# Seven weight loads move from SP's DMA queue to GpSimd's, in a kernel whose order is set by a planner

## The chip, the cores and the metric

One core of one Trainium2 chip. The metric is the device time of one execution in microseconds; the kernel before takes 885.57 us (median of three runs, 884.84 to 885.59).

## The reference, cut to what matters

```python
# q, k, v: (8 batches, 8 heads, 576 positions, 64); w_in: (512, 2048); w_out: (2048, 512); all float32
scores = scale * np.matmul(q_c, k_c.transpose(0, 1, 2, 4, 3))      # chunks of 64 positions
scores = scores - np.max(scores, axis=-1, keepdims=True)
attn = np.exp(scores)
attn = attn / (np.sum(attn, axis=-1, keepdims=True) + 1e-09)
x = np.matmul(attn, v_c)                                           # then to (4608 tokens, 512)
h = x @ w_in
g = np.maximum(h, 0.0) + np.log1p(np.exp(-np.abs(h)))              # softplus
return g @ w_out
```

## The kernel before, in words

The 4608 tokens are 36 pairs of chunks (128 tokens each), and four pairs make an m-tile of 512 tokens; there are nine. Each m-tile runs 16 blocks, one for each 128 of the 2048 hidden columns. Block g has a first GEMM G1_g (x times w_in, 12 matmuls, line 527), softplus and a split of the result into a high and a low part (`sp`, `hi`, `lo`: ACT at lines 538 and 542, then DVE or POOL at line 546), and a second GEMM G2_g (12 matmuls, line 560). TensorE (PE) runs them as G1_0, G1_1, G2_0, G1_2, G2_1 and so on. A float32 product is made of three matmuls over high and low parts, so the weights are split too.

A weight unit u is 128 hidden columns of w_in or of w_out: units 0 and 1 are w_in of blocks 0 and 1, and then they alternate (unit 2 is w_out of block 0, unit 3 w_in of block 2, unit 4 w_out of block 1, and so on). Each of the 32 units takes this way: `load` (512 KB by DMA, lines 228 and 233) into one of three `raw` buffers; `w_top` (ACT or POOL, line 239) and `w_low` (ACT, line 248), which read the raw buffer and free it; `w_add` (DVE, line 253); `w_hi` (ACT or POOL, line 274); `w_lo` (DVE or POOL, line 278). A w_in unit has to be ready for G1 of its block, a w_out unit for G2.

Attention is made in two ways. The first four pairs (`q0` to `v3`, line 305, with PE transposes) come ahead of G1_0, which needs `xl3`, the last of them (DVE, line 507). The others come in bursts of PE work between blocks: B3, B8 and B15 in the first m-tile, in two halves each, then two bursts in each m-tile. A burst needs for its two pairs q and k (line 404, eight DMAs of 32 KB each, then DVE transposes `Tq`, `Tk` at line 412), and for the pairs before it `v` (line 314, four DMAs) and `swap` (line 445, eight DMAs from SBUF to SBUF, after softmax).

The order on every engine is fixed when the program is built, and each engine works through its own list and waits at an entry until what this needs is there. The class `Plan` sets the order: it plays the tasks through with a cost for each, and at each moment takes the task with the lowest `urg`. All DMAs before go through SP's queue. They take eight semaphores in turn, so a DMA on SP also waits until the eighth before it has landed; the planner before knows this only as at most five loads under way (`FLYING`).

```python
LOAD_AFTER = "v0"                       # when the first weight load may be ordered
can = [t for t in wait[eng] if ready[t["name"]] <= now + 1e-9 and has_room(t, now)]
t = min(can, key=lambda t: (t["urg"], t["seq"]))
before = dict(zip(seq[1:], seq))        # PE: G1_g follows G2_(g-2), or the burst
```

Of the kernel before, what the change touches and what calls it, by code (L numbers as in the profile page):

```python
# [16 lines left out]
F16 = mybir.dt.float16  # L17
# [16 lines left out]
class Plan:  # L34
# [6 lines left out]
    FLYING = 5  # L41
# [6 lines left out]
    def add(  # L48
        self, name, eng, cost, fn, needs=(), urg=0.0, table=None, take=(), kb=0, slack=0.0, after=(), port=False
    ):  # L50
        self.tasks[name] = dict(
            name=name, eng=eng, cost=cost, fn=fn, needs=list(needs) + list(after), after=set(after), urg=urg, table=table,
            take=take, kb=kb, slack=slack, seq=len(self.tasks), port=port or eng == "POOL",
        )

    def order(self):
# [7 lines left out]
        wait, flying = {}, []  # L64
# [28 lines left out]
        while times:  # L93
# [3 lines left out]
            flying = [e for e in flying if e > now]  # L97
# [45 lines left out]
def chunked_attention_softplus_ffn(  # L143
# [92 lines left out]
    def w_top(u):
        top = tops[u % TOP_BUFS].bitcast(F16).rearrange("p (f t) -> p f t", t=2)[:, :, 1]
# [340 lines left out]
    T0, TG = 18.0, 5.5  # L578
    TK = (0,2)
# [33 lines left out]
    for u, (g, is_in, fc) in enumerate(units):  # L613
# [23 lines left out]
        plan.add(last[0], ph_, 0.65 if ph_ == "POOL" else 0.53, partial(w_hi, u, is_in, fc),  # L637
# [39 lines left out]
    for at, (pv, ps) in bursts.items():  # L677
# [19 lines left out]
        for i in (a, b):  # L697
            for n, src in (("q", q), ("k", k)):
# [6 lines left out]
                plan.add(f"{n}{i}", "SP", 4.2, partial(blk_load, i, n, src), free, urg=d - QK_URG, kb=256,  # L705
# [4 lines left out]
        for n in range(2):  # L710
            i = a + n
            free = [] if ps == F else [nxt[n]]
            plan.add(f"v{i}", "SP", 2.8, partial(blk_v_load, i), free, urg=d - V_URG, kb=256,
# [11 lines left out]
            plan.add(f"swap{i}", "SP", 5.0, partial(blk_swap, i), [f"Te{i}"] + gone, urg=d - SW_URG, kb=256)  # L725
# [68 lines left out]
```

## Time and profile before

| what | value |
|---|---|
| median of three runs | 885.57 us |
| the profiled execution | 883.88 us |
| its span, first to last instruction | 882.0 us |
| PE busy in the span | 861.7 us (98%) |
| ACT, DVE, POOL busy | 316.8, 329.8, 56.1 us |
| mean granted TensorE clock | 0.998 |
| moved by DMA | 63.91 MB, 72 GB/s over the span |

The profiled execution is 1.69 us below the median; 1.9 us of it lie outside the span. Busy shares are means over the whole span: the first 130 us, in which the weights are loaded and split, have other limits than the rest.

### The profile page before, as it was taken

How to read it: one execution, taken by the hardware profiler on the slowest of the kernel's cores; microseconds unless marked ns; L12 is line 12 of the kernel's file. 1: busy time of each engine (PE TensorE's matmuls, PEld its weight loads, DVE VectorE, ACT ScalarE, POOL GpSimd, SP SyncE). 2: the span in 40 equal slices, each digit the busy share in tenths (PEclk: the TensorE clock that was granted, in tenths of full speed). 3: DMA queues.
4: the chain of work that ended last, by engine and by line, in shares of the span. 5: the costliest groups of instructions: out<-in, count | busy, mean ns of one | idle time of the engine just before them, and what ended most of it. 6: DMA issues, size and time to landing. Idle time of an engine off the chain costs nothing.

```text
span 882.0 us, 14812 instructions
## 1 busy us (share of the span) xinstructions
PE 861.7 (98%) x5868; PEld 700.9 (79%) x5868; DVE 329.8 (37%) x550; ACT 316.8 (36%) x494; POOL 56.1 (6%) x58
## 2 busy tenths in 40 slices
PE   8699989999999999999999999999999999999998
PEld 7577878888888888888888888888888888888886
DVE  5667854333415251524233432334153414121111
ACT  4677763232424242324232422333232423232222
POOL 1353630000000000000000000000000000000000
PEclk9999999999999999999999999999999999999999
DMA  9676763313232324132412232232223231000001
GB/s 224 171 200 201 208 149 92 62 39 63 41 86 40 63 41 100 28 64 41 105 30 46 52 62 74 41 66 42 81 39 63 44 94 31 18 18 31 1 1 48
DMA packets 214852, 63.91 MB, mean 72 GB/s; under 512 B 191744, under 2 KB 208128, under 8 KB 214784
## 3 DMA queue, kind: packets, MB, share of 16 engines
q1 hardware_dynamic: 214784, 62.98, 31.7%
q8 instruction: 46, 0.75, 0.4%
q14 instruction: 22, 0.18, 0.1%
HBM read 45.09 MB, written 9.44 MB: 62 GB/s over the span
## 4 chain that ended last, share of the span: by engine, by line
PE 87%; DMA 6%; SPq 2%; ACT 2%; POOL 1%; issue 1%; DVE 1%; DVEq 0%; ACTq 0%; POOLq 0%
PE po L560 43%; PE pa L527 41%; DMA raw<-in_moe_w_out_dram 3%; PE pa L491 2%; DMA raw<-in_moe_w_in_dram 2%; PE pa L424 2%; SPq L305 1%; DMA q<-in_q_dram 1%; ACT top L239 0%; SPq L228 0%; POOL top L239 0%; ACT low L248 0%; ACT u L538 0%; DMA k<-in_v_dram 0%; DVE low L253 0%
## 5 line engine op out<-in xcount | busy, mean ns | idle before, releaser
L538 ACT ACTIVATE u<-pa 128x512 f32<-128x512 f32 x144 | 86.0, 597 | 498.5 <-PE pa L527 498.4
L546 DVE TENSOR_TENSOR g_lo<-u,g_hi 128x512 fp32r<-128x512 f32 x136 | 94.6, 695 | 356.7 <-ACT g_hi L542 356.3
L527 PE MATMUL pa<-x,wib 128*128 128x512 f32 x864 | 208.7, 390 | 1.9 <-DVE wib L278 1.9
L527 PEld LDWEIGHTS pa<-x,wib 128*128 128x128 f32 x864 | 161.6, 188 | 38.1 <-DVE wib L278 2.3
L527 PE MATMUL pa<-x,wi_hi 128*128 128x512 f32 x576 | 178.0, 390 | 1.4 <-DVE x L507 1.4
L560 PE MATMUL po<-late,g_hi 128*128 128x512 f32 x540 | 172.1, 394 | 0.0
L527 PEld LDWEIGHTS pa<-x,wi_hi 128*128 128x128 f32 x576 | 108.1, 188 | 24.1 <-DVE x L507 1.8
L560 PEld LDWEIGHTS po<-late,g_hi 128*128 128x128 f32 x540 | 101.2, 187 | 24.4
L560 PE MATMUL po<-wo_hi,g_lo 128*128 128x512 f32 x288 | 115.6, 401 | 3.1 <-DVE g_lo L546 3.1
L560 PE MATMUL po<-late,g_lo 128*128 128x512 f32 x288 | 114.6, 398 | 0.0
L560 PE MATMUL po<-wo_lo,g_hi 128*128 128x512 f32 x288 | 114.4, 397 | 0.0
L560 PE MATMUL po<-wo_hi,g_hi 128*128 128x512 f32 x288 | 113.8, 395 | 0.0
L527 PE MATMUL pa<-x,wi_lo 128*128 128x512 f32 x288 | 112.8, 392 | 0.0
L542 ACT CAST g_hi<-u 128x512 fp32r<-128x512 f32 x144 | 89.2, 619 | 4.4
L560 PEld LDWEIGHTS po<-wo_hi,g_lo 128*128 128x128 f32 x288 | 54.4, 189 | 16.5 <-DVE g_lo L546 3.3
L527 PEld LDWEIGHTS pa<-x,wi_lo 128*128 128x128 f32 x288 | 54.0, 188 | 14.1 <-PE po L560 2.8
L560 PEld LDWEIGHTS po<-wo_hi,g_hi 128*128 128x128 f32 x288 | 54.4, 189 | 13.4
L560 PEld LDWEIGHTS po<-wo_lo,g_hi 128*128 128x128 f32 x288 | 54.4, 189 | 12.8
L560 PEld LDWEIGHTS po<-late,g_lo 128*128 128x128 f32 x288 | 54.0, 187 | 13.1
L455 DVE TENSOR_REDUCE mx<-pa 128x8 f32<-128x512 f32 x32 | 22.0, 686 | 70.0 <-ACT x L503 68.5
L412 DVE STREAM_TRANSPOSE ka<-k 128x512 f32<-128x512 f32 x30 | 21.3, 710 | 52.8 <-DMA k<-in_k_dram 42.5
L471 DVE TENSOR_REDUCE den<-qe 128x8 f32<-128x512 f32 x32 | 21.1, 660 | 16.6 <-ACT qe L466 16.6
(97 smaller groups left out, 546.0 us busy)
## 6 DMA issues: line engine op xcount, KB each, us to landing
out_dram<-raw SPq DMA_DIRECT2D x36, 256.0 KB, 2.6
raw<-in_moe_w_in_dram SPq DMA_DIRECT2D x16, 512.0 KB, 4.6
raw<-in_moe_w_out_dram SPq DMA_DIRECT2D x16, 512.0 KB, 4.5
eT<-ka SPq DMA_DIRECT2D x256, 32.0 KB, 1.9
q<-in_q_dram SPq DMA_DIRECT2D x240, 32.0 KB, 2.1
k<-in_k_dram SPq DMA_DIRECT2D x240, 32.0 KB, 2.1
q<-in_v_dram SPq DMA_DIRECT2D x60, 64.0 KB, 2.4
k<-in_v_dram SPq DMA_DIRECT2D x60, 64.0 KB, 2.4
```

The lines of the kernel that those rows point to most:

```text
L305: eng.dma_start(dst[p0 : p0 + rows], src[b, :, s0 : s0 + rows, :].rearrange("h s d -> s h d"))
L412: nc.vector.transpose(t, live.pop((n, i)))
L424: nc.tensor.matmul(pa[o, c2, col : col + C], qT[r, a * HP + hl, :], kT[r, a * HP + hl, :], start=True, stop=True,)
L455: nc.vector.tensor_reduce(mx, sc, axis=AX.X, op=ALU.max)
L471: nc.vector.tensor_reduce(den, e, axis=AX.X, op=ALU.add)
L491: nc.tensor.matmul(pa[o, a, col : col + C], vt[r, 4 * j + 2 * h2 + c2, :], eT(r, c2, j, h2), start=True, stop=True,)
L527: nc.tensor.matmul(ph, wt[:, c, fs], x[:, :, c, :], start=(n == 0), stop=(n == 3 * KC - 1))
L538: nc.scalar.activation(w["u"], w["ph"], AF.Softplus)
L542: nc.scalar.copy(w["hi"], w["u"])
L546: (nc.gpsimd if pool else nc.vector).tensor_tensor(w["lo"], w["u"], w["hi"].bitcast(F32), op=ALU.subtract)
L560: nc.tensor.matmul(pos[w["m"]][t], gg[:, ts_], wt, start=(w["first"] and n == 0), stop=(w["last"] and n == 2),)
```

## The change

Units 2, 3, 4, 5, 7, 9 and 11 are loaded by a DMA that POOL (GpSimd) issues, on a queue of its own with semaphores of its own; the other 25 stay on SP. No load is ordered ahead of `v3` now (before: `v0`). The planner models the main queue anew: eight lanes, in which a DMA waits until the eighth before it has landed, each of the several DMAs of a task by itself (`parts`), and a limit on how far issues run ahead of the data (`AHEAD`). Costs and due times of many tasks are set anew, and with them the lists of who does which part of a unit. The two `top` buffers are handed out in the order of use. The second burst of the later m-tiles comes at block 14 (before 13).

```diff
-    FLYING = 5
+    FLYING = 8
+    AHEAD = 3.2
...
-                if free.get(eng, 0.0) > now + 1e-9 or eng == "SP" and len(flying) >= self.FLYING:
+                if free.get(eng, 0.0) > now + 1e-9:
...
+                last = end
+                if t["kb"]:
+                    end, lanes = now, landed.setdefault(eng, [0.0] * self.FLYING)
+                    for _ in range(t["parts"]):
+                        end = max(end, lanes[-self.FLYING] + 0.1, dma_free - self.AHEAD) + cost / t["parts"]
+                        dma_free = max(end + 1.0, dma_free) + t["kb"] * 1024 / self.RATE / t["parts"]
+                        lanes.append(max(dma_free + 0.8, end + 1.6))
+                    last = lanes[-1]
...
-                if t["kb"]:
-                    dma_free = max(now + 1.8, dma_free) + t["kb"] * 1024 / self.RATE
-                    end = max(dma_free + 0.8, end + 2.0)
-                    flying.append(end)
+                end = last
...
     def w_load(u, is_in, fc):
+        queue = nc.gpsimd if u in LOAD_POOL else nc.sync
...
-    T0, TG = 18.0, 5.5
-    TK = (0,2)
+    T0, TG = 30.0, 5.2
+    TK = (3,)
...
+    LOAD_POOL = (2,3,4,5,7,9,11)
...
-    LOAD_AFTER = "v0"
+    LOAD_AFTER = "v3"
...
-    NORM_POOL = (0,1,3,4,5)
+    NORM_POOL = (0,1,4,7)
...
-    V_AFTER = "load16"
-    K6_AFTER = "load2"
+    V_AFTER = "load10"
+    K6_AFTER = "load8"
...
-        plan.add(f"load{u}", "SP", 0.6, partial(w_load, u, is_in, fc), urg=d - LEAD if u else LQ, kb=490,
+        pool = u in LOAD_POOL
+        plan.add(f"load{u}", "POOL" if pool else "SP", 1.0 if pool else 0.55, partial(w_load, u, is_in, fc),
+                 urg=d - LEAD if u else LQ, kb=440,
                  take=[("raw", [f"w_top{u}", f"w_low{u}"])], after=[LOAD_AFTER])
```

The order of SP's queue before, from `v0` on (raw_174, 248, 269, 361, 418 and 426 are the loads of units 0, 1, 2, 3, 4 and 5; q_295 and k_367 are q and k of pair 4):

```order
L305 DMA late_104<-in_v_dram 128x8x64
L228 DMA raw_174<-in_moe_w_in_dram 128x4x512
L305 DMA late_111<-in_v_dram 128x8x64
L305 DMA late_118<-in_v_dram 128x8x64
L305 DMA eT_123<-in_v_dram 128x8x64
L228 DMA raw_248<-in_moe_w_in_dram 128x4x512
L233 DMA raw_269<-in_moe_w_out_dram 128x2048
L404 DMA q_295<-in_q_dram 32x8x32 x8
L228 DMA raw_361<-in_moe_w_in_dram 128x4x512
L404 DMA k_367<-in_k_dram 32x8x32 x8
L233 DMA raw_418<-in_moe_w_out_dram 128x2048
L228 DMA raw_426<-in_moe_w_in_dram 128x4x512
```

The same place in the changed kernel (raw_222 and raw_241 are units 0 and 1, raw_428 is unit 6, raw_530 unit 8; q_287, k_391 and the two x_96 are q and k of pairs 4 and 5):

```order
L313 DMA late_104<-in_v_dram 128x8x64
L313 DMA late_111<-in_v_dram 128x8x64
L313 DMA late_118<-in_v_dram 128x8x64
L313 DMA eT_123<-in_v_dram 128x8x64
L234 DMA raw_222<-in_moe_w_in_dram 128x4x512
L234 DMA raw_241<-in_moe_w_in_dram 128x4x512
L412 DMA q_287<-in_q_dram 32x8x32 x8
L412 DMA k_391<-in_k_dram 32x8x32 x8
L239 DMA raw_428<-in_moe_w_out_dram 128x2048
L412 DMA x_96<-in_q_dram 32x8x32 x8
L412 DMA x_96<-in_k_dram 32x8x32 x8
L239 DMA raw_530<-in_moe_w_out_dram 128x2048
```

Units 2 to 5 have left the queue, unit 0 stands behind all four v instead of behind the first, and q and k of pairs 4 and 5 follow each other with one weight load between the pairs.

SP's queue ahead of the burst B8, before (x_97 of v is v of pairs 4 and 5; eT is the swap of pair 4, then of pair 5; raw_763 to 941 are units 13 to 19):

```order
L228 DMA raw_763<-in_moe_w_in_dram 128x4x512
L233 DMA raw_767<-in_moe_w_out_dram 128x2048
L445 DMA eT_795<-ka_462 32x256 x8
L228 DMA raw_850<-in_moe_w_in_dram 128x4x512
L233 DMA raw_854<-in_moe_w_out_dram 128x2048
L228 DMA raw_857<-in_moe_w_in_dram 128x4x512
L445 DMA eT_859<-ka_568 32x256 x8
L233 DMA raw_908<-in_moe_w_out_dram 128x2048
L314 DMA x_97<-in_v_dram 64x4x64 x4
L228 DMA raw_941<-in_moe_w_in_dram 128x4x512
L314 DMA x_97<-in_v_dram 64x4x64 x4
```

And in the changed kernel (raw_712 is unit 12, raw_740 to 891 are units 13 to 18, in order):

```order
L239 DMA raw_712<-in_moe_w_out_dram 128x2048
L322 DMA x_97<-in_v_dram 64x4x64 x4
L234 DMA raw_740<-in_moe_w_in_dram 128x4x512
L322 DMA x_97<-in_v_dram 64x4x64 x4
L239 DMA raw_773<-in_moe_w_out_dram 128x2048
L412 DMA x_97<-in_k_dram 32x8x32 x8
L234 DMA raw_832<-in_moe_w_in_dram 128x4x512
L239 DMA raw_834<-in_moe_w_out_dram 128x2048
L453 DMA eT_837<-ka_462 32x256 x8
L234 DMA raw_888<-in_moe_w_in_dram 128x4x512
L239 DMA raw_891<-in_moe_w_out_dram 128x2048
L453 DMA eT_906<-ka_565 32x256 x8
```

The two v loads, which came behind both swaps, now come ahead of them and of k of pair 7.

POOL's list after the identity matrix is made, before (late and x by den: norm of pairs 0, 1 and 3; top: `w_top` of units 2 to 5):

```order
L478 TENSOR_TENSOR late_102<-late_102,den_204 128x512
L478 TENSOR_TENSOR late_109<-late_109,den_274 128x512
L278 TENSOR_TENSOR wi_lo_90<-wib_91,wi_hi_89 128x4x128
L239 CAST top0_98<-raw_269 128x512
L478 TENSOR_TENSOR x_96<-x_96,den_388 128x512
L239 CAST top1_99<-raw_361 128x512
L278 TENSOR_TENSOR wi_lo_90<-wib_91,wi_hi_89 128x4x128
L239 CAST top1_99<-raw_426 128x512
```

And in the changed kernel (raw_224, 342, 407, 490 and 502 are the loads of units 2, 3, 4, 5 and 7):

```order
L239 DMA raw_224<-in_moe_w_out_dram 128x2048
L486 TENSOR_TENSOR late_102<-late_102,den_237 128x512
L486 TENSOR_TENSOR late_109<-late_109,den_296 128x512
L234 DMA raw_342<-in_moe_w_in_dram 128x4x512
L247 CAST top1_99<-raw_224 128x512
L247 CAST top0_98<-raw_241 128x512
L239 DMA raw_407<-in_moe_w_out_dram 128x2048
L286 TENSOR_TENSOR wi_lo_90<-wib_91,wi_hi_89 128x4x128
L282 CAST wo_hi_93<-wib_91 128x512
L286 TENSOR_TENSOR wi_lo_90<-wib_91,wi_hi_89 128x4x128
L247 CAST top1_99<-raw_342 128x512
L234 DMA raw_490<-in_moe_w_in_dram 128x4x512
```

The loads stand among the casts and subtractions of POOL's list. The first waits for nothing; each later one waits until its raw buffer has been read by ACT and by POOL, and what is behind it in the list waits with it. The norm of pair 3 has gone to DVE.

## Rows read from the trace of the kernel before

**Rows 1.** The page, part 1: busy time, share of the span, instructions.

```profile
PE 861.7 (98%) x5868; PEld 700.9 (79%) x5868; DVE 329.8 (37%) x550; ACT 316.8 (36%) x494; POOL 56.1 (6%) x58
```

**Rows 2.** The windows view: stretch, length, busy PE, PEld, DVE, ACT, POOL; clock, DMA share, GB/s.

```profile
131.70:882.00 750.30, 746.65 (x4827) 605.80 (x4824) 244.49 (x421) 233.16 (x359) 3.44 (x3) 1.00 0.24 51
```

**Rows 3.** The timeline of PE: start, length, instruction, idle before it and releaser.

```profile
31.21 0.73 PE L527 MATMUL pa<-x,wi_hi 128*128 128x512 f32 x2 [1.44 <-DVE x L507]
...
40.22 0.79 PE L560 MATMUL po<-wo_hi,g_lo 128*128 128x512 f32 x1 [3.08 <-DVE g_lo L546]
...
44.69 0.40 PE L527 MATMUL pa<-x,wi_lo 128*128 128x512 f32 x1
...
86.07 1.06 PE L491 MATMUL pa<-eT,x 64*64 64x64 f32 x29 [2.07 <-issue]
...
125.65 3.04 PE L527 MATMUL pa<-x,wib 128*128 128x512 f32 x12 [1.89 <-DVE wib L278]
...
130.68 0.51 PE L491 MATMUL pa<-eT,k 64*64 64x64 f32 x19 [0.48 <-DMA k<-in_v_dram]
```

**Rows 4.** The windows view, the four microseconds after the longest wait of PE.

```profile
40.00:44.00 4.00, 3.78 (x10) 3.00 (x11) 3.34 (x5) 2.02 (x4) 2.00 (x2) 0.57 0.71 203
```

**Rows 5.** The chain that ended last, two blocks without a wait.

```profile
137.47 2.79 PE po L560 x12
...
140.26 2.73 PE pa L527 x12
```

**Rows 6.** The timeline of SP's DMA queue: start, length, issues of one line merged.

```profile
16.95 0.60 SPq L233 DMA_DIRECT2D raw<-in_moe_w_out_dram  x1
...
23.45 3.96 SPq L404 DMA_DIRECT2D k<-in_k_dram  x8
...
52.23 5.24 SPq L404 DMA_DIRECT2D x<-in_q_dram  x8
...
70.43 7.06 SPq L445 DMA_DIRECT2D eT<-ka  x8
...
81.55 2.58 SPq L314 DMA_DIRECT2D x<-in_v_dram  x4
...
96.63 5.71 SPq L445 DMA_DIRECT2D eT<-ka  x8
...
126.06 2.57 SPq L314 DMA_DIRECT2D k<-in_v_dram  x4
```

**Rows 7.** The waits of SP's queue, 0 to 130 us: total, times, longest.

```profile
SPq L404 <- DMA raw<-in_moe_w_out_dram: 5.8, 5, 2.2
SPq L404 <- DMA raw<-in_moe_w_in_dram: 5.8, 6, 1.8
```

**Rows 8.** Line 228, the weight loads of w_in: issue in ns, landing in us.

```profile
L228 SPq DMA_DIRECT2D raw<-in_moe_w_in_dram x16: 372/392/1897, 9.7 to 115.4; - x16
...
DMA to landing us min/median/max: 4.0/4.6/7.1
```

**Rows 9.** The timeline of ACT.

```profile
21.60 0.78 ACT L239 CAST top<-raw 128x512 f16<-128x512 bf16 x1
...
22.72 0.63 ACT L466 ACTIVATE x<-x 128x512 f32<-128x512 f32 x1
...
33.04 0.78 ACT L239 CAST top<-raw 128x512 f16<-128x512 bf16 x1 [1.84 <-DMA raw<-in_moe_w_out_dram]
...
35.84 1.28 ACT L538 ACT_TABLE_LOAD   x1
...
37.13 0.60 ACT L538 ACTIVATE u<-pa 128x512 f32<-128x512 f32 x1
```

**Rows 10.** The timeline of DVE ahead of the first GEMM.

```profile
29.26 0.71 DVE L412 STREAM_TRANSPOSE ka<-k 128x512 f32<-128x512 f32 x1 [1.73 <-DMA k<-in_k_dram]
...
30.47 0.68 DVE L507 TENSOR_TENSOR x<-pa,x 128x512 fp32r<-128x512 f32 x1
```

**Rows 11.** The timeline of POOL: the same cast alone and beside DVE.

```profile
22.99 0.76 POOL L239 CAST top<-raw 128x512 f16<-128x512 bf16 x1
...
39.55 1.24 POOL L239 CAST top<-raw 128x512 f16<-128x512 bf16 x1 [3.00 <-DMA raw<-in_moe_w_out_dram]
```

More of the change, by code (lines that the diff above doesn't have):

```diff
@@ L48, in add @@
     def add(
-        self, name, eng, cost, fn, needs=(), urg=0.0, table=None, take=(), kb=0, slack=0.0, after=(), port=False
+        self, name, eng, cost, fn, needs=(), urg=0.0, table=None, take=(), kb=0, slack=0.0, after=(), port=False, parts=1
     ):
@@ L52, in add @@
             name=name, eng=eng, cost=cost, fn=fn, needs=list(needs) + list(after), after=set(after), urg=urg, table=table,
-            take=take, kb=kb, slack=slack, seq=len(self.tasks), port=port or eng == "POOL",
+            take=take, kb=kb, slack=slack, seq=len(self.tasks), port=port or eng == "POOL", parts=parts,
         )
@@ L63, in order @@
         fin, issued, free, tab, dma_free, port = {}, {}, {}, None, 0.0, 0.0
-        wait, flying = {}, []
+        wait, landed = {}, {}
         times = [0.0]
@@ L227, in w_load @@
         if is_in:
-            nc.sync.dma_start(
+            queue.dma_start(
                 st.rearrange("p (c f) -> p c f", c=KC),
@@ L232, in w_load @@
         else:
-            nc.sync.dma_start(st, w_out_v[:, fc, :])
+            queue.dma_start(st, w_out_v[:, fc, :])
         live["raw", u] = raw
     def w_top(u):
-        top = tops[u % TOP_BUFS].bitcast(F16).rearrange("p (f t) -> p f t", t=2)[:, :, 1]
+        live["top", u] = tops[0]
+        tops.append(tops.pop(0))
+        top = live["top", u].bitcast(F16).rearrange("p (f t) -> p f t", t=2)[:, :, 1]
         src = live["raw", u].bitcast(BF16)[:, 4:].rearrange("p (f t) -> p f t", t=4)[:, :, 0]
@@ L252, in w_add @@
         low = live["low", u]
-        nc.vector.tensor_tensor(low, low, tops[u % TOP_BUFS], op=ALU.add)
+        nc.vector.tensor_tensor(low, low, live.pop(("top", u)), op=ALU.add)
     def w_parts(u, is_in, fc):
@@ L636, in chunked_attention_softplus_ffn @@
             freed.append(f"w_hi{(of_in if is_in else of_out)[fc - 1]}")
-        plan.add(last[0], ph_, 0.65 if ph_ == "POOL" else 0.53, partial(w_hi, u, is_in, fc),
+        plan.add(last[0], ph_, 0.63 if ph_ == "POOL" else 0.61, partial(w_hi, u, is_in, fc),
                  [f"w_add{u}"] + users + freed, urg=d + 2.1)
@@ L704, in chunked_attention_softplus_ffn @@
                     free = [f"T{n}{a - 2}" if ps <= F + 2 else f"B{prev}_{'qk'.index(n)}"]
-                plan.add(f"{n}{i}", "SP", 4.2, partial(blk_load, i, n, src), free, urg=d - QK_URG, kb=256,
+                plan.add(f"{n}{i}", "SP", 4.0, partial(blk_load, i, n, src), free, urg=d - QK_URG, kb=420, parts=8,
                          after=[QK_AFTER if ps == F else K6_AFTER])
@@ L712, in chunked_attention_softplus_ffn @@
             free = [] if ps == F else [nxt[n]]
-            plan.add(f"v{i}", "SP", 2.8, partial(blk_v_load, i), free, urg=d - V_URG, kb=256,
+            plan.add(f"v{i}", "SP", 2.4, partial(blk_v_load, i), free, urg=d - V_URG, kb=310, parts=4,
                      after=[V_AFTER])
@@ L724, in chunked_attention_softplus_ffn @@
             gone = [f"V{FIRST_BLK - 1}"] if ps == F else [f"B{at}_{n}"]
-            plan.add(f"swap{i}", "SP", 5.0, partial(blk_swap, i), [f"Te{i}"] + gone, urg=d - SW_URG, kb=256)
+            plan.add(f"swap{i}", "SP", 4.4, partial(blk_swap, i), [f"Te{i}"] + gone, urg=d - SW_URG, kb=190, parts=8)
         prev = at
```

31 lines of the change are left out of this document (15 added, 16 removed).

## The prediction

> **What bounds the kernel now.** The page comes first: PE is busy for 98% of the span [rows 1], so time can only be won where PE waits or where its work is stretched. The windows view shows where that isn't: from 131.70 us to the end PE is busy for 746.65 of 750.30 us [rows 2], and the missing 3.65 us are the last copies and stores. A block without a wait costs 2.79 + 2.73 us in the chain [rows 5], and nothing in the change touches that. The later bursts come at even distances of eight blocks instead of seven and nine; seven blocks were enough without a wait, so eight are. So the forecast is the moment at which the burst B15 ends, 131.70 us, and everything behind it is taken as it was.
>
> The third view is PE's timeline ahead of that moment [rows 3]. G1_0 runs from 31.21, as `xl3` is done then. G2_0 waits 3.08 us for DVE's `g_lo` and starts at 40.22. The window behind it has a granted clock of 0.57 [rows 4], near the lower of the two levels (1.2 and 2.4 GHz); before it PE had stood still. G2_0 ends at 44.69, so it takes 4.47 us instead of 2.79, and 1.68 us go to the clock. B8's second half stands 2.07 us until 86.07, G1_15 1.89 us until 125.65, B15's second half 0.48 us until 130.68.
>
> Behind these waits is SP's queue. Its timeline is a closed row of issues from the start to 128.63 [rows 6]: eight small DMAs take 3.96 us behind one weight load, 5.24 behind two; a swap takes 7.06 behind three and 5.71 behind two; four v DMAs take 2.58. The waits view says why [rows 7]: eleven times a q or k load stood, 11.6 us in all, because the eighth DMA before it was a weight load that had not landed. Such a load takes only 0.39 us to issue but 4.6 to land [rows 8]. B8's second half started 1.94 us after the v row at 81.55 had been issued (84.13), B15's second half 2.05 us after the one at 126.06 (128.63): these two were late v loads.
>
> **The change, part by part.** The sum goes along time; p is what one load costs POOL.
>
> *Up to G1_0.* Unit 2's load, the first thing on POOL, moves 512 KB beside the first q and k; unit 0's, which stood behind the first v, goes behind the last. Ahead of the last v there are as many bytes as before. Unit 0's now takes the place that unit 1's had, and unit 1's that of unit 2's, issued by 17.55 [rows 6]. Unit 1's cast ran on ACT at 21.60, when ACT came free [rows 9]; I put the new first cast at 20.9. ACT's new order has `exp` of pair 3 behind it: cast, `w_low`, `xh0` and two copies at some 0.55 each, so 23.6, where it ran at 22.72 [rows 9]. From its end at 24.2 DVE has 1.1 us of `den` and eight operations at some 0.62 ahead of `xl3`, which starts at about 30.3 against 30.47 [rows 10]; the 1.73 us that DVE stood for k of pair 4 then are filled by its own work. G1_0 starts at 31.0: 0.2 us won, no more.
>
> *G2_0.* Before, ACT did the first softplus only at 37.13, as two units stood ahead of it on ACT's list and the cast at 33.04 had waited 1.84 us for its data, and a table load of 1.28 stood between [rows 9]. Now units 3 and 4 come by POOL. Unit 3's load may go when ACT has read unit 0's buffer, at 22.1; behind it stand p, two casts at 0.8, and p again, so unit 4's data are there at 22.1 + 1.6 + 2p + 4.6 = 28.3 + 2p. The trace of before has no DMA on POOL. From below p is bounded by SP's 0.39; from above no row bounds it. The nearest rows are POOL's own cast, 0.76 alone and 1.24 beside DVE [rows 11], and I take 1.2, as DVE is hardly idle here. That gives 30.7; four operations of ACT (2.6), the table load (1.28), softplus, `w_hi4` and `g_hi` (1.7) and DVE's 0.68 make 37.0. G1_0 and G1_1 end at 31.0 + 5.46 = 36.5. G2_0 starts at 37.0, half a microsecond behind PE, at the full clock, and ends at 39.8: 4.9 us earlier than 44.69 (0.2 from G1_0, 3.0 from the wait and its filler, 1.7 from the clock).
>
> *B8.* The v loads of pairs 4 and 5 now come before both swaps in SP's order, so the 2.07 us go; the swaps come last. SP by its rows: 17.55 + 5.2 (q of pair 4 behind two loads) + 3.9 + 0.5 + 7.8 + 0.5 + 11.7 + 1.0 + 2.6 + 0.5 + 2.6 + 0.5 + 3.9 + 1.0 = 59.2 up to the first swap, then 5.7 + 1.0 + 5.7 = 71.6, landed by 76. PE comes to B8's second half at 39.8 + (86.07 - 44.69 - 2.07) = 79.1. So B8 doesn't wait, and is 7.0 us earlier.
>
> *B15.* SP goes on with three loads (1.5), q (7.0), two loads (1.0), k (5.2) and a load, and is at the swap of pair 6 at 86.8. But that swap needs the softmax of B8: it was issued at 96.63, 10.56 us after 86.07. So now it goes at 89.7, and SP stands for 2.9 us. From there to the end of the last v load lay 32.0 us (96.63 to 128.63), for the same issues in nearly the same order; so 121.7, and with 2.05 us to the data B15's second half starts at 123.7. PE alone could be there at 130.68 - 4.9 - 2.07 - 1.89 - 0.48 = 121.3 (G1_15's wait was for a `w_lo` on DVE behind a k transpose, and DVE's new order has it ahead). SP's queue is later and decides: 130.68 - 123.7 = **7.0 us won**. The profiled execution, 883.88, would come to 876.9; it lies 1.69 us below the median, and against the median of 885.57 the forecast is **878.6 us**.
>
> *What p does.* Unit 8's load on SP needs a buffer that POOL's cast of unit 6 frees, and this cast stands behind four loads. The third of them may go when ACT has read unit 3's buffer, two reads (1.25) after 28.3 + 2p; two loads and the cast (0.8) later it is 30.4 + 4p, where SP is there at 35.0. Unit 10's cast has two loads and 6.9 us of POOL's own work more ahead: 37.3 + 6p, against 47.2. With p = 1.2 neither matters; up to about 1.8 SP's 2.9 us of standing hide it; beyond, each us of p costs 4 to 6 us, as all of SP's q, k, v and swaps wait behind these loads. The edits to the `top` buffers and the lists of ACT, DVE and POOL for later units move work of 0.6 to 1.3 us between engines that are not full in 40 to 130 us, and I cost them at nothing; if that cover is gone, a wait like G1_15's 1.89 us comes back for each.
>
> A rule of the Trainium skill speaks against p = 1.2: by "SBUF — State Buffer", "Who interferes with whom", descriptors of a DMA from GpSimd are written through a port that some DVE operations lock, and its section on the bandwidth-pool intuition gives some 620 ns alone and 3100 ns beside a DVE copy. No run here shows it yet; with p = 3.1 the sum would be: unit 10 at 37.3 + 18.6 = 55.9, SP 8.7 late, the swap of pair 6 at 95.5, 1.1 us won.
>
> **The rivals.**
>
> *Only issue time is saved.* Seven loads leave a queue that pays 0.39 us for each [rows 8]: 2.7 us, 882.9. For it: the same bytes go through the same 16 DMA engines, and POOL's loads can push SP's small DMAs back as much as they did when they stood among them. Against it: the 11.6 us of waits [rows 7] are for semaphores that SP alone uses. The Trainium skill, "DMA: Bandwidth & Descriptors", "Issuing engines are not separate DMA queues", states this rival.
>
> *Nothing is won.* The first GEMM starts as before by my own walk, and what G2_0 wins can be given back at B8 or B15, if SP's swaps and v loads come no earlier than they did. That needs 9.9 us more on SP than I add up (7.0 and the 2.9 of standing): 885.6.
>
> *Slower: POOL's list blocks SP.* The place is SP's load of unit 10 (unit 8 in a lesser way), the price 6 us for each us of p above 1.65, the turning point p = 3.3 (37.3 + 19.8 - 47.2 = 9.9). With p = 4 unit 10 waits until 61.3, SP is 14.1 late, the last v load is issued at 133: 4.4 us lost, 890. For it: the cast row stretches from 0.76 to 1.24 beside DVE [rows 11], so POOL does pay for DVE's work. Against it: 3.3 is 2.7 times the longer of these two.
>
> **How the numbers follow.** The likeliest, 0.52: p below 2, SP's queue as added up, 5 to 9.3 us won, 876.3 to 880.6, middle 878.6. Only issue time, or a part of the sum lost to a new wait (1.8 to 5 us won): 0.20. Nothing: 0.12. Slower: 0.16. A measurement of this kernel can tell about 0.2%, 1.8 us, from no change. So faster 0.72, same 0.12, slower 0.16. The range takes in the likeliest case up to PE alone with an earlier first GEMM (10.8 us won, 874.8), the smaller gain and no change, and reaches a little into the slower case: 874.8 to 886.8.
>
> **What the profile of the changed kernel would show.** G1_0 between 30 and 32 us. G2_0 within 1 us of G1_1's end, no window with a low clock behind it. POOL's loads at about 1.2 us in its queue. No wait in B8; B15's second half at 121 to 125, released by a v load. SP at the swap of pair 6 with a few us of standing, released by DVE. It is wrong if SP stands at unit 8 or 10 for POOL, if G1_0 comes after 33 (ACT standing at the first cast), or if PE waits at other blocks between B3 and B15 for weights that SP now issues later.

## The result: half a per cent slower

The changed kernel takes 888.63 us (median of 16 runs, 885.45 to 892.24), the kernel before 884.84 in the same rounds (16 runs, 881.26 to 885.96). The ratio is 1.0047, with an interval of 1.0033 to 1.0062: 3.8 us slower, where 7.0 us of gain were forecast. The range, which ended at 886.8, doesn't hold the time either.

The profiled execution of the changed kernel took 891.1 us (span 889.3), 2.5 us above its median; its rows show where the time goes, the size comes from the medians. The page, part 1 and two of its DMA queues (packets, MB, share of 16 engines):

```profile
PE 868.4 (98%) x5872; PEld 705.1 (79%) x5872; DVE 325.7 (37%) x545; ACT 314.7 (35%) x491; POOL 71.0 (8%) x73
...
q1 hardware_dynamic: 211856, 59.31, 30.1%
q0 software_dynamic: 1008, 3.67, 1.4%
```

The second queue, POOL's, moved 3.67 MB: the seven loads. PE's timeline at the places of [rows 3] (G1_0, G2_0, G2_4, B8's second half, B15's second half):

```profile
35.02 0.73 PE L535 MATMUL pa<-x,wi_hi 128*128 128x512 f32 x2 [2.26 <-DVE x L515]
...
42.24 0.50 PE L568 MATMUL po<-wo_hi,g_lo 128*128 128x512 f32 x1 [1.27 <-DVE g_lo L554]
...
69.09 0.79 PE L568 MATMUL po<-wo_hi,g_lo 128*128 128x512 f32 x1 [2.87 <-POOL g_lo L554]
...
89.65 0.83 PE L499 MATMUL pa<-eT,x 64*64 64x64 f32 x29
...
133.68 0.30 PE L499 MATMUL pa<-eT,k 64*64 64x64 f32 x2 [1.35 <-DMA k<-in_v_dram]
...
135.52 0.98 PE L499 MATMUL pa<-eT,k 64*64 64x64 f32 x27 [1.54 <-DMA k<-in_v_dram]
```

G1_0 comes 3.8 us later than before, G2_0 2.0 later. The wait for `v` in B8 is gone, but two new ones have come: 2.87 us at G2_4, for POOL, and 2.89 us in all at B15, for the last v. The windows view of three stretches (columns as in [rows 2]):

```profile
66.13:74.37 8.24, 5.38 (x13) 4.13 (x13) 3.50 (x4) 4.31 (x8) 7.39 (x6) 0.64 0.86 221
130.00:140.00 10.00, 7.10 (x141) 5.61 (x140) 4.79 (x8) 3.58 (x7) 1.27 (x1) 0.83 0.52 117
137.22:889.30 752.08, 747.93 (x4825) 606.63 (x4824) 242.38 (x419) 233.66 (x360) 5.17 (x4) 1.00 0.24 51
```

Each of the two new waits has a low granted clock with it (0.64 and 0.83 as means, between the levels of 1.2 and 2.4 GHz). From the end of B15 the rest takes 752.08 us, 1.8 more than before [rows 2]. So 5.5 of the 7.3 us by which this execution's span is longer lie ahead of 137.22 us (131.70 before), the stretch in which the forecast had looked for its gain. SP's queue, its rows of q and k up to 57 us, the first swap, the swap of pair 6, unit 31 and the last v:

```profile
18.16 6.34 SPq L412 DMA_DIRECT2D q<-in_q_dram  x8
24.55 3.93 SPq L412 DMA_DIRECT2D k<-in_k_dram  x8
...
29.02 6.57 SPq L412 DMA_DIRECT2D x<-in_q_dram  x8
35.63 5.38 SPq L412 DMA_DIRECT2D x<-in_k_dram  x8
...
41.60 4.75 SPq L412 DMA_DIRECT2D q<-in_q_dram  x8
46.45 4.92 SPq L412 DMA_DIRECT2D k<-in_k_dram  x8
51.42 5.44 SPq L412 DMA_DIRECT2D x<-in_q_dram  x8
...
71.07 5.79 SPq L453 DMA_DIRECT2D eT<-ka  x8
...
101.83 4.96 SPq L453 DMA_DIRECT2D eT<-ka  x8
...
128.89 0.55 SPq L239 DMA_DIRECT2D raw<-in_moe_w_out_dram  x1
129.61 2.58 SPq L322 DMA_DIRECT2D k<-in_v_dram  x4
```

Seven loads have left this queue, and it is later: the swap of pair 6 at 101.83 instead of 96.63, the last v at 129.61 instead of 126.06 [rows 6]. Of the 7.3 us, 3.55 are that issue, 1.3 the later landing behind it (3.3 us from the last issue to PE's start, before 2.05), and the other 2.5 lie behind that start, most of them at the low clock around and behind B15. SP's waits up to 130 us (total, times, longest):

```profile
SPq L412 <- DMA raw<-in_moe_w_in_dram: 5.3, 5, 1.8
SPq L239 <- ACT low L256: 4.6, 4, 1.7
SPq L412 <- DMA raw<-in_moe_w_out_dram: 3.3, 4, 1.0
SPq L412 <- DMA x<-in_q_dram: 1.7, 2, 1.4
SPq L412 <- DMA k<-in_k_dram: 1.5, 1, 1.5
SPq L412 <- DMA q<-in_q_dram: 1.4, 2, 1.2
```

The q and k rows still stand 8.6 us for loads (before 11.6, [rows 7]), and now 4.6 us for earlier DMAs of q and k themselves (before 0.4): 13.2 us in all. The waits have changed what they wait for; they aren't shorter. Another 4.6 us are new: w_out loads that wait for ACT to read their buffer. POOL's timeline, three of its seven loads and the place at G2_4:

```profile
1.45 0.71 POOL L239 DMA_DIRECT2D raw<-in_moe_w_out_dram  x1
...
23.37 0.81 POOL L234 DMA_DIRECT2D raw<-in_moe_w_in_dram  x1 [3.04 <-ACT wib L256]
...
44.85 0.77 POOL L234 DMA_DIRECT2D raw<-in_moe_w_in_dram  x1
...
66.63 1.21 POOL L247 CAST top<-raw 128x512 f16<-128x512 bf16 x1 [4.93 <-DMA raw<-in_moe_w_in_dram]
67.78 1.26 POOL L554 TENSOR_TENSOR g_lo<-u,g_hi 128x512 fp32r<-128x512 f32 x1
```

The loads cost POOL 0.55 to 0.81 us each. But the cast of unit 13 stands 4.93 us for its data, and `g_lo` of block 4, for which PE waits, is behind it. ACT's timeline at the first weight cast, then DVE's at `xl3` and at `g_lo` of block 0:

```profile
21.77 0.77 ACT L247 CAST top<-raw 128x512 f16<-128x512 bf16 x1 [2.62 <-DMA raw<-in_moe_w_in_dram]
```

```profile
33.08 0.71 DVE L420 STREAM_TRANSPOSE ka<-k 128x512 f32<-128x512 f32 x1 [2.12 <-DMA x<-in_q_dram]
...
34.28 0.68 DVE L515 TENSOR_TENSOR x<-pa,x 128x512 fp32r<-128x512 f32 x1
...
40.90 0.71 DVE L420 STREAM_TRANSPOSE qe<-x 128x512 f32<-128x512 f32 x1 [3.62 <-DMA x<-in_k_dram]
41.54 0.65 DVE L554 TENSOR_TENSOR g_lo<-u,g_hi 128x512 fp32r<-128x512 f32 x1
```

Both times DVE stands at a transpose of a later pair, which needs SP's small DMAs, while an entry close behind it (`xl3`, then `g_lo`) is what PE waits for.

### The profile page after: what moved, and what is told of

Read it like the earlier page. It is cut to its first block, busy times and chain, and to the rows that moved or that the text cites. A ratio compares the mean times of both kernels' runs of the same rounds, so it can differ in the third digit from the quotient of the medians.

```text
span 889.3 us, 14833 instructions
## 1 busy us (share of the span) xinstructions
PE 868.4 (98%) x5872; PEld 705.1 (79%) x5872; DVE 325.7 (37%) x545; ACT 314.7 (35%) x491; POOL 71.0 (8%) x73
## 3 DMA queue, kind: packets, MB, share of 16 engines
q0 software_dynamic: 1008, 3.67, 1.4%
## 4 chain that ended last, share of the span: by engine, by line
PE 90%; DMA 3%; SPq 3%; issue 1%; DVE 1%; ACT 1%; POOL 0%; ACTq 0%; POOLq 0%
PE po L568 44%; PE pa L535 42%; PE pa L499 2%; SPq L313 2%; PE pa L432 2%; DMA raw<-in_moe_w_in_dram 1%; SPq L412 1%; DMA k<-in_k_dram 1%; DMA k<-in_v_dram 1%; DMA raw<-in_moe_w_out_dram 1%; SPq L322 0%; DMA x<-in_k_dram 0%; ACT u L546 0%; ACT L546 0%; POOL g_lo L554 0%
## 5 line engine op out<-in xcount | busy, mean ns | idle before, releaser
L554 DVE TENSOR_TENSOR g_lo<-u,g_hi 128x512 fp32r<-128x512 f32 x131 | 89.2, 681 | 289.9 <-ACT g_hi L550 287.0
L568 PEld LDWEIGHTS po<-late,g_lo 128*128 128x128 f32 x288 | 54.4, 189 | 13.2
L420 DVE STREAM_TRANSPOSE qe<-q 128x512 f32<-128x512 f32 x30 | 21.2, 705 | 70.2 <-DMA k<-in_k_dram 49.8
```

The source lines that it names most:

```text
L420: nc.vector.transpose(t, live.pop((n, i)))
L554: (nc.gpsimd if pool else nc.vector).tensor_tensor(w["lo"], w["u"], w["hi"].bitcast(F32), op=ALU.subtract)
L568: nc.tensor.matmul(pos[w["m"]][t], gg[:, ts_], wt, start=(w["first"] and n == 0), stop=(w["last"] and n == 2),)
```

## The experiments

Two theories were set against each other, and both against "the second queue itself does harm". *Order*: the loss comes from the new order of the lists, whatever queue the loads are on. *Shared engines*: POOL's loads push SP's small DMAs back, because both use the same 16 DMA engines; its rival is *semaphores in turn*, by which the prediction walked SP's queue (only loads on SP itself delay SP's rows). Where a program "moves" entries, it takes one out of the finished order and puts it behind another. Ratios are to the kernel before in the same rounds; "v7" is the time at which SP or POOL had issued the last v of B15. The last two columns come from one profiled execution each: e1's is its fastest, 3.1 us under its median, the changed kernel's lies 2.5 us above.

| run | ratio and interval | v7 issued | profiled span |
|---|---|---|---|
| before | 1 | 128.63 | 882.0 |
| changed | 1.0047 (1.0033 to 1.0062) | 132.19 | 889.3 |
| e1_all_sp | 1.0067 (1.0045 to 1.0089) | 130.60 | 885.8 |
| e2_before_pool | 1.0008 (0.9993 to 1.0023) | 130.20 | 883.8 |
| e4_glo_dve | 1.0029 (1.0012 to 1.0045) | 129.83 | 886.3 |
| e5_moves | 1.0069 (1.0046 to 1.0091) | 133.05 | 891.0 |
| e6_v7_first | 1.0037 (1.0020 to 1.0054) | 128.61 | 887.0 |
| e7_all_moves | 1.0048 (1.0029 to 1.0067) | 128.32 | 887.5 |
| e8_quarter | 0.9999 (0.9979 to 1.0019) | 127.16 | 885.1 |
| e9_before_v7 | 1.0091 (1.0074 to 1.0108) | 128.93 | 890.4 |
| e10_before_v_pool | 1.0028 (1.0004 to 1.0052) | 131.75 | 886.7 |
| e11_after_v_pool | 1.0043 (1.0026 to 1.0060) | 133.17 | 890.2 |
| e12_all_v_pool | 1.0032 (1.0016 to 1.0049) | 131.19 | 886.9 |
| e13_load0_early | 1.0021 (1.0000 to 1.0043) | 129.92 | 886.9 |
| e14_load2_later | 1.0021 (0.9998 to 1.0043) | 129.42 | 884.8 |
| e15_all_order | 0.9996 (0.9977 to 1.0015) | 127.52 | 882.5 |
| e16_before_quarter | 0.9951 (0.9930 to 0.9972) | 125.08 | 878.2 |

### The queue by itself

The changed kernel with all loads on SP, and the kernel before with the same seven on POOL:

```diff
-        queue = nc.gpsimd if u in LOAD_POOL else nc.sync      # e1, on the changed kernel
+        queue = nc.sync
```

```diff
+        queue = nc.gpsimd if u in (2, 3, 4, 5, 7, 9, 11) else nc.sync      # e2, on the kernel before
-            nc.sync.dma_start(
+            queue.dma_start(
```

> The changed kernel with its order kept entry for entry, but the seven loads issued by SP where they stand. Theory A (the loads share the 16 engines wherever they are issued, and the loss comes from the new order): q and k of pair 4 land as late as in the changed kernel, and the time stays within 2 us of it (887 to 891), plus at most 2.7 us of issue. Theory B (GpSimd's own queue does harm, by getting its bytes ahead of SP's small DMAs or by its descriptors): SP's small DMAs land sooner again, G1_0 comes back by 2 us or more, and the time falls to 886 or below. Theory C (the prediction's, semaphore lanes): slower than the changed kernel by 3 to 8 us, since SP waits for seven loads more.

> The kernel before with its order kept, and units 2, 3, 4, 5, 7, 9, 11 issued by GpSimd where they stand in its program. Theory A: within 2 us of the kernel before (883 to 887). Theory B: slower by 2 us or more (887 and up), with eight DMAs on SP taking 5 us or more where they took 3.9 to 4.2 behind one load. Theory C: faster by 3 to 7 us (878 to 882), with SP's queue ahead by some microseconds at the first swap.

With the old order the second queue makes no difference (1.0008), and without it the new order is no better (1.0067; its interval overlaps that of the changed kernel). So the loss in time is in the order and not in the queue. The time of both came out as the first theory of their expectations had it. But G1_0 sides with the second theory: in e1 it starts at 32.02, 3.0 us ahead of the changed kernel (e6, the earliest trace with the same lists up to there, has 34.39). And in e2 PE's timeline, at G1_0 and at B15's second half, shows the same the other way round:

```profile
36.83 1.22 PE L528 MATMUL pa<-x,wi_hi 128*128 128x512 f32 x2 [4.25 <-DVE x L508]
...
131.70 0.79 PE L492 MATMUL pa<-eT,k 64*64 64x64 f32 x29
```

G1_0 is 5.6 us later than in [rows 3], B15's second half only 1.0: the waits that the kernel before has at G2_0, B8, G1_15 and B15 are shorter or gone in e2, and so take up a late front.

*Semaphores in turn* had SP's rows shrink when loads leave SP. They don't: the seven rows of q and k take 34.8 us before and 35.3 in e2, 34.8 in e1 and 37.3 in the changed kernel. In the new order the first swap stays where it is, at 71.07 or, with all loads on SP (e1):

```profile
70.70 5.52 SPq L453 DMA_DIRECT2D eT<-ka  x8
```

And in e2's waits the small DMAs have taken much of the loads' place, as in the changed kernel (7.1 us with 0.8 for `x`, and 5.4 for loads; 12.5 in all, 12.0 before):

```profile
SPq L405 <- DMA k<-in_k_dram: 3.2, 3, 1.2
SPq L405 <- DMA q<-in_q_dram: 3.1, 3, 1.6
```

The start of SP's queue shows the sharing with no semaphore in play, as its first eight DMAs wait for none. The fifth of them, in the chain view of the kernel before and in SP's timeline of the changed kernel:

```profile
3.80 1.14 SPq L305
```

```profile
4.57 2.75 SPq L313 DMA_DIRECT2D late<-in_q_dram  x1
```

In the nine traces in which POOL issues unit 2's load at 1.45 us, this one issue takes 2.73 to 3.67 us, and SP comes to the first v at 9.96 to 10.96 us. In the eight others, three of them with the changed kernel's order (e1, e14, e15), it takes 0.92 to 1.81, and the first v goes at 8.38 to 8.94.

### Bytes or semaphores

The same cut in both kernels: six loads bring a quarter of their unit, and the casts read that quarter four times over. So those weights aren't the reference's; orders, DMA counts and sizes of the casts stay.

```diff
+        part = 4 if u in (3, 4, 5, 7, 9, 11) else 1      # e8 changed kernel, e16 kernel before
...
-                st.rearrange("p (c f) -> p c f", c=KC),
-                w_in_v[:, :, 4 * fc * P : 4 * (fc + 1) * P],
+                st.rearrange("p (c f) -> p c f", c=KC)[:, : KC // part],
+                w_in_v[:, : KC // part, 4 * fc * P : 4 * (fc + 1) * P],
```

> The changed kernel, but POOL's loads of units 3, 4, 5, 7, 9 and 11 bring only a quarter of the unit (128 KB instead of 512), which the casts then read four times over, so that those weights are not the reference's; order, number of DMAs and work of all engines stay. Theory 'shared engines' (POOL's bytes lengthen the landing of SP's small DMAs): SP's rows of eight between 20 and 60 us take about 4 us instead of 4.75 to 6.57, the load of unit 10 is issued 4 to 6 us earlier than 57.4, the first swap 3 us or more earlier than 71.07, and the time falls to 885 or 886 where the casts don't hold it. Rival 'semaphores in turn' (SP's rows are set by their own small DMAs and the loads on SP alone, as the prediction walked them): the rows of q and k keep their length within 0.3 us, the first swap stays at 70 to 71.5, and the time at 888 to 889.

> The kernel before, in its own order and all on SP, but the loads of units 3, 4, 5, 7, 9 and 11 bring only a quarter of the unit (128 KB), which the casts read four times over, so that those weights are not the reference's. It is the control for the same cut made in the changed kernel (which gave 0.9999 of the kernel before, 4 us below the changed kernel). Theory 'shared engines': the kernel before too is held by bytes in its first 60 us, its rows behind those loads shrink from 4 to 5 us to about 4, the first swap is issued 3 to 5 us earlier than 63.64, and the time falls by 1 to 4 us, 881 to 884, as far as waits at B8 and B15 let it. Rival 'semaphores in turn': fewer bytes don't matter where each load is one of eight DMAs in turn; the rows and the first swap stay within 1 us, and the time within 0.15% of the kernel before.

SP's queue in e8, the rows that answer to those of the changed kernel above:

```profile
29.37 4.11 SPq L420 DMA_DIRECT2D x<-in_q_dram  x8
33.53 4.25 SPq L420 DMA_DIRECT2D x<-in_k_dram  x8
...
66.58 5.03 SPq L461 DMA_DIRECT2D eT<-ka  x8
...
124.58 2.58 SPq L330 DMA_DIRECT2D k<-in_v_dram  x4
```

The row at 29 us falls from 6.57 to 4.11 us, the next from 5.38 to 4.25, the seven rows together from 37.3 to 32.5. The first swap is 4.5 us earlier, v7 5.0. These sizes are loose: in six other traces with the same SP queue up to there (e4 to e7, e11, e12) the seven rows take 33.9 to 38.6 us and the first swap comes at 69.16 to 72.32, so e8 lies below all of them, but by 1.4 us at least and 6.1 at most. The cut loads are on POOL's queue, with POOL's semaphores; what reaches SP's rows can only be what both queues share. So *semaphores in turn* falls and *shared engines* holds, though these runs don't tell the engines from the memory behind them. And in e16:

```profile
60.94 5.53 SPq L453 DMA_DIRECT2D eT<-ka  x8
...
122.51 2.57 SPq L322 DMA_DIRECT2D k<-in_v_dram  x4
```

The first swap is 2.7 us earlier than before (63.64), v7 3.55 [rows 6], and the time falls by 0.49%, more than expected. The two cuts give the same, 4.2 us from the changed kernel's ratio and 4.3 from the kernel before: as far as intervals of about 0.2% tell, the order's loss and the bytes' price add up.

### The entries that hold PE

In e4 `g_lo` of blocks 4 and 5 goes from POOL to DVE. In e5 the two transposes that held DVE go behind what PE waited for. In e13 and e14, both with e4's edit, a load is moved; e15 has all of it, with unit 31's load and its reads on ACT moved too.

```diff
-partial(sp_lo, w, pool)                           # e4, and in e6, e7, e12 to e15
+partial(sp_lo, w, pool and g not in (4, 5))
...
+MOVES = (("Tk4", "xl3"), ("Tq5", "lo0"))          # e5: entry, and the entry behind which it goes
+MOVES = (("load0", "v0"),)                        # e13
+MOVES = (("load2", "norm0"),)                     # e14
+MOVES = (("load2", "norm0"), ("Tk4", "xl3"), ("Tq5", "lo0"), ("load31", "v7"),
+         ("w_top31", "xh7"), ("w_low31", "w_top31"))      # e15
```

> The changed kernel, with the low parts of g of blocks 4 and 5 made by DVE instead of POOL, at the same place of the program. If POOL's list (a cast of unit 13 that waits for its data, ahead of g_lo of block 4) costs what the profile shows at G2_4 (2.87 us of standing and 2.5 us at a low clock), the profile shows neither, and the time falls by 2 to 5 us, to 884 to 887, less what is then lost at B15, where SP's v load is late anyway. If POOL's list only stands in front of a wait that another engine would cause, the time stays within 1 us of the changed kernel.

> The changed kernel, with DVE's transposes of k of pair 4 and of q of pair 5 moved behind xl3 and behind g_lo of block 0, so that DVE does not stand for late q and k loads. If that standing is what delays G1_0 and G2_0: G1_0 starts at 32.5 to 33.5 (35.0 in the changed kernel), G2_0 at 38 to 39.5 (42.2). Whether the time falls tells what comes behind: if the stop at G2_4 and the late v load set the end, less than 1.5 us of it is left (887 to 889); if not, 884 to 886.

> The changed kernel with g_lo of blocks 4 and 5 on DVE (887.6 by itself) and the load of unit 0 issued behind v of pair 0 instead of behind v of pair 3, as in the kernel before. It measures the step of the prediction that has unit 0 come no later for its new place. Theory 'unit 0 is late': ACT's first cast comes at 20 or 21 instead of 21.8 with 2.6 us of standing, G1_0 starts at 32 to 33 instead of 35.0 to 35.9, and G2_0 about 2 us earlier; the time falls by 1 to 2 us to 885.5 to 886.5 if nothing behind takes it back. Rival 'unit 2 is in front' (POOL's first load, 512 KB beside the first q and k, is what makes everything late): the first k, PE's first transposes and G1_0 stay within 0.7 us of where they are, 887 to 888.

> The changed kernel with g_lo of blocks 4 and 5 on DVE (887.6 by itself), and POOL's load of unit 2 behind the norm of pair 0 in POOL's list (about 15 us) instead of first. Theory 'unit 2 is in front' (its 512 KB move beside the first q and k and make the whole front late): DVE's first operation comes at 10.2 instead of 11.3 to 11.7, G1_0 starts 1 to 1.5 us earlier than 35.9, at about 34.5, and the time is 886 to 887. Rival 'the bytes only move' (they now lie beside v and q of pair 4): DVE's first operation at 10.2, but Tk4 on DVE stands as long or longer and G1_0 is not earlier than 35; 887.5 or more.

> The changed kernel with every list entry moved that held PE in its trace: unit 2's load behind the norm of pair 0, Tk4 behind xl3, Tq5 behind g_lo of block 0, g_lo of blocks 4 and 5 on DVE, unit 31's load behind v of pair 7, and ACT's reads of unit 31 behind xh of pair 7. Theory 'the order is the loss': no wait over 1 us behind G1_0; B15's second half at 129 to 130.5, 882 to 884. Rival 'supply' (swaps, buffers and v come on SP no earlier than in the kernel before): B15 waits for v7, B15's second half at 131 or later, 885 to 886.5, so as fast as the kernel before and no faster.

PE's timeline of e5 at G2_0 and G2_4:

```profile
38.95 0.50 PE L577 MATMUL po<-wo_hi,g_lo 128*128 128x512 f32 x1 [0.46 <-DVE g_lo L563]
69.50 0.79 PE L577 MATMUL po<-wo_hi,g_lo 128*128 128x512 f32 x1 [6.60 <-POOL g_lo L563]
```

The two moves win 3.3 us at G2_0, and G2_4 gives all of it back (69.50 against 69.09): its wait grows from 2.87 to 6.60 us, since POOL's cast of unit 13 waits for SP. e5's G1_0 (32.49) and G2_0 came as expected, its time didn't. With e4 alone this wait is gone and the ratio falls to 1.0029, less than expected; the two intervals overlap. e13 shows that unit 0's place wasn't what made the front late: its cast comes at 19.20, but G1_0 at 36.1, with DVE standing 3.87 us at Tk4, as its rival had it. In e14, with unit 2 no longer in front, DVE's first TENSOR_REDUCE is at 9.95 (changed kernel 11.70, before 10.16). But G1_0, at 34.5, is no earlier than in e6 (34.39), where unit 2 is in front, so for G1_0 this settles nothing. With all of it, e15, PE's timeline at G2_4 and at B15's second half, and SP's at v7:

```profile
65.43 0.51 PE L577 MATMUL po<-wo_hi,g_lo 128*128 128x512 f32 x1 [2.12 <-DVE g_lo L563]
...
129.50 0.51 PE L508 MATMUL pa<-eT,k 64*64 64x64 f32 x19 [0.32 <-DMA k<-in_v_dram]
```

```profile
124.95 2.57 SPq L331 DMA_DIRECT2D k<-in_v_dram  x4
```

The loss is gone (0.9996), and nothing is won, though 882 to 884 us were expected; 885.61 came (884.5 by the ratio). B15's second half is 1.2 us earlier than in [rows 3], but from there to the end of the span it takes 753.0 us instead of 751.3; at 65.43 PE also has a wait of 2.12 us, for DVE now, that wasn't to be there. So the order explains the loss; but mending these entries doesn't turn the second queue into a gain. How the 3.8 us divide among the moved entries isn't settled: the intervals of e4, e13 and e14 overlap.

### The tail

Here unit 31 goes behind v7 (e6, e7, e9), or v goes to POOL's queue (pairs 6 and 7 in e11 and e12, 4 to 7 in e10).

```diff
+MOVES = (("load31", "v7"),)                                        # e6, with e4's edit
+MOVES = (("Tk4", "xl3"), ("Tq5", "lo0"), ("load31", "v7"))         # e7, with e4's edit
+MOVES = (("Tk9", "w_lo29"), ("load31", "v7"))                      # e9, on the kernel before
...
+        queue = nc.gpsimd if 6 <= i < 8 else nc.sync               # v_load: e11, e12; e10 with 4 <= i
-                nc.sync.dma_start(
+                queue.dma_start(
```

e10, on the kernel before, also has Tk9 behind `w_lo29`; e12 has e4's edit, e5's moves and those of ACT's reads of unit 31.

> The changed kernel with two entries moved: g_lo of blocks 4 and 5 on DVE (as in the run before with only that, 887.6), and the load of unit 31 issued behind v of pair 7 instead of directly ahead of it. Theory 'the order in the tail' (the last v load lands late because 512 KB were put directly ahead of it): v7 starts 0.6 us earlier and its data are there 2.0 us behind its last issue instead of 3.3, so B15's second half starts about 131.2 and the time is 885.4 to 886.2. Rival 'supply' (SP's row as a whole is late, what stands directly ahead doesn't matter): v7's data come within 0.5 us of where they were, 887 to 888. Second rival: unit 31, now 3 us later, is itself waited for at G2_15; then PE shows a wait there released by POOL's w_lo and the time is 887 or more.

> The changed kernel with all the list entries moved that were seen to hold PE: Tk4 behind xl3, Tq5 behind g_lo of block 0, g_lo of blocks 4 and 5 on DVE, unit 31's load behind v7. Theory 'the order is the loss': G1_0 at 32, G2_0 at 39, no wait at G2_4, v7 not behind a load, and the 3 us won early are kept: 881 to 883, below the kernel before. Rival 'supply': what is won ahead of B8 is given back as a wait for v7 at B15, because SP's row depends on when buffers and bytes come and not on PE; then B15's second half stays at 131 to 132 and the time at 885 to 886.5, with a wait of 3 to 5 us at B15.

> The kernel before (no load on POOL, its own order) with two entries moved: Tk of pair 9 on DVE behind w_lo of unit 29, and unit 31's load behind v of pair 7. It asks for a version better than both. Theory 'the order in the tail': G1_15's 1.89 us of waiting for w_lo29 goes, v7 is issued 0.4 us earlier or more unless the later Tk9 holds its buffer; B15 ends 0.5 to 2 us earlier: 882.5 to 884. Rival 'supply': the wait moves from G1_15 to B15's second half and the time stays within 0.1% of 884.7.

> The kernel before, its weight loads all on SP, with the small DMAs of v of pairs 4 to 7 (four each) issued by POOL instead, and Tk of pair 9 on DVE moved behind w_lo of unit 29. It asks for a version better than both: what is late in the kernel before is v, so v goes to the second queue and not the weights. Theory 'order in one queue' (v was late only because it stood behind SP's long row): B8's 2.07 us, G1_15's 1.89 and B15's 0.48 of waiting go, 4.4 us in all: 880 to 881.5. Rival 'shared engines' (the data of v come no earlier than the 16 engines give them): at least half of the waits stay and the time is 883 to 885. Rival 'POOL pays': four small DMAs and their wait for a buffer hold up POOL's g_lo of block 7 or its parts of units 15 to 18 and 30, new waits of PE released by POOL appear, 885 or more.

> The changed kernel with the DMAs of v of pairs 6 and 7 issued by POOL; nothing else differs. Theory 'order in one queue' (the end of B15 in the changed kernel is set by v7 at the end of SP's row): v7 is issued when Tk9 has freed its buffer, B15's 2.9 us of waiting go and B15's second half comes at about 132.6 instead of 135.5: 885.5 to 886.5 against 888.6 of the changed kernel. Rival 'shared engines': unit 31 and the rest still hold v7's data back, B15 waits at least 1.5 us: 887.5 to 889.

> The changed kernel with g_lo of blocks 4 and 5 on DVE, Tk4 behind xl3, Tq5 behind g_lo of block 0, v of pairs 6 and 7 issued by POOL, and ACT's two reads of unit 31 behind xh of pair 7 (where the version with unit 31 behind v7 stood on ACT and made G1_16 wait 2.4 us). Theory 'the order is the loss': no wait at G2_4, at B15 or at G1_16; B15 ends at 130.5 to 131.5 and the time is 882 to 884, a little below the kernel before. Rival 'supply' (weights and swaps come as late as in the changed kernel): waits at other blocks between B8 and B15 take up what is won and the time is 885.5 to 888.

In all six the theory that the run was made for missed. By their ratios e6, e10, e11 and e12 come out about where a rival had them; of *POOL pays* in e10 only the number came, as PE's new waits there are for v's data. e7 and e9 are slower than any theory had them. That unit 31 stood directly ahead of v7 isn't what made v7 land late: in e6, with the load behind, the wait ends 3.7 us after the last issue; in e14, with the load ahead, 2.0. And a load that is moved takes its readers along. ACT's timeline of e9:

```profile
135.08 0.76 ACT L248 CAST top<-raw 128x512 f16<-128x512 bf16 x1 [9.13 <-DMA raw<-in_moe_w_out_dram]
```

ACT stands 9.13 us at unit 31's cast, which its list has ahead of the softplus of block 15; PE then waits 7.63 us. In e6 and e7 the same cast is ahead of `xh` of pair 6; ACT stood there 4.71 and 4.55 us, and in e7 G1_16 waited 2.40 us behind it. On POOL four v DMAs cost 2.43 to 2.61 us, as on SP, but v7 is issued no earlier: it needs the buffer that Tk9 on DVE frees (Tk9 starts at 126.3 to 128.3 us in these three), Tk9 needs k of pair 9, and k is in SP's row. In e11 and e12 a `g_lo` of 1.74 us stands ahead of v7 on POOL as well. With v7 on SP the distance is as short: in the changed kernel, e4, e6 and e15 its row starts 0.2 to 0.9 us behind the end of Tk9. So v7 hangs on k of pair 9, whichever queue it stands in. What is won early doesn't reach it: e12's G2_0 comes 4.7 us earlier than e4's (38.94 against 43.64), its last wait for v7 ends 0.5 later (133.59 against 133.09).

## Why the prediction was wrong

*The step that failed* is the walk of SP's queue, "59.2 up to the first swap": it was issued at 71.07. Of these 11.9 us, 8.7 are the seven rows of q and k, forecast at 28.6 in all (5.2, and 3.9 for each further one) and measured at 37.3; 0.6 is the later start, 1.0 the row of k of pair 7 (4.94 for 3.9), the rest mostly loads that waited. The 3.9 came from one row with one load ahead [rows 6]; in the kernel before the seven rows take 34.8. I took it that loads on another queue cost these rows nothing. e1 and e2 show that they cost no less there than on SP. e8 shows a part of the price, 4.8 us between two traces (1.4 to 6.1 over the others) for three quarters of six loads; even its rows are 3.9 us above the forecast. All the later terms were hung on this one: the swap of pair 6 at 89.7 (101.83), v7 issued by 121.7 (132.19), B15's second half at 123.7 (135.52).

*Up to G1_0*, 31.0 forecast, 35.02 measured, past the 33 that was named as a sign of being wrong. "Ahead of the last v there are as many bytes as before" left out that unit 2's lie beside the first q and k: SP comes to the first v 1.0 us later at least. What that costs at G1_0 no run singles out; all seven loads on POOL cost 3.0 us there (e1). The order of DVE's list behind that, Tk4 ahead of `xl3`, was counted as DVE "filled by its own work"; it stood 2.12 us there.

*G2_0*, 37.0 forecast, 42.24 measured. Right: no low clock behind it, G1_2 follows 2.9 us later as at the full clock. Wrong: Tq5 stands ahead of `g_lo` on DVE, again for SP's small DMAs.

*p*, taken as 1.2 us: measured 0.55 to 0.81. The 0.76 of [rows 11] was read as a cast alone, but DVE was busy from 22.84 to 24.13 in that trace; so the two rows don't show what DVE's work costs POOL. The third rival, POOL's list blocking SP, didn't come about, though its 890 is the price nearest to the measured time. The rule of the Trainium skill that was weighed there ("SBUF — State Buffer", "Who interferes with whom") doesn't show in this case: DVE is busy for 28.86 of the 40 us from 20 to 60, no load takes POOL over 0.81 us, and POOL's loads land in 4.6 to 6.2 us where SP's take 3.6 to 6.6. DVE ran no copy while POOL issued them, so the figure for a copy isn't tested here.

*B8*: the wait for v is gone, as forecast. But its 2.07 us are lost elsewhere: B8's second half comes at 89.65 (forecast 79.1, before 86.07).

*The lists*, "I cost them at nothing": the text named the price of a lost cover, 1.89 us, and G2_4 cost 2.87 and a low clock. This cover wasn't checked entry by entry: POOL's cast of unit 13 was put ahead of `g_lo`, and SP issues that unit at 61.26 us, where the walk, up to behind the first v, had 50.8.

*The rest* behind B15 as it was: right to 1.8 us in 750.

Of the rivals, *nothing is won* had the mechanism ("SP's swaps and v loads come no earlier than they did"), and *only issue time is saved* had the cause, the same 16 engines. The Trainium skill ("DMA: Bandwidth & Descriptors", "Issuing engines are not separate DMA queues") says that DMAs run on the same 16 engines whichever engine started them, and that issuing from several saves only issue time; e2 (1.0008) and e8 (0.9999) agree with it. The forecast weighed the 11.6 us of waits for semaphores [rows 7] against it. Those waits were real; but what they wait for is landing, and landing is slowed from both queues. No case put the loss where it came from: entries that wait for a DMA, ahead of entries that PE waits for (e15). Whether the planner chose them because its rows are too short wasn't tested.

## What to carry to other kernels

A wait for a semaphore of a DMA is a wait for its landing: before moving transfers to another queue, ask whether fewer bytes would shorten it. A kernel whose front runs on one closed row of DMAs can give back, at the end of that row, what is won ahead of it, as e12 did; so find the last transfer of the row and what it hangs on. And where a change writes the lists anew, look in each list for an entry that waits for a DMA and stands close ahead of one that the main engine waits for.

## What was not expected of the hardware

POOL issues a 512 KB load in 0.55 to 0.81 us beside a busy DVE, and four small v DMAs in 2.43 to 2.61 us, against 2.58 on SP. One load of 512 KB on POOL's queue makes a single issue on SP's take 2.73 to 3.67 us instead of 0.92 to 1.81, though that issue waits for no semaphore. Six loads cut by 2.3 MB (six times 384 KB) are worth 0.48 to 0.49% of an 885 us kernel, although the DMA share from 20 to 60 us is only 0.80 in the changed kernel (0.69 with the cut) and 0.75 in the kernel before (0.63). That share isn't bounded by 1: it is 1.35 from 8 to 12 us in the kernel before.
